# Joining the last steps of a decode kernel to its loop, turning w3 into a moving operand, and sharing semaphores

## The chip, the cores and the metric

The kernel runs on one core of a Trainium2 chip. The profile names its engines PE (TensorE, matrix products; PEld is its loading of weights), DVE (VectorE), ACT (ScalarE), POOL (GpSimd) and SP (SyncE, which issues the loads here); 16 DMA engines move the data. The metric is device time in microseconds (us): the median of repeated executions, of which one per kernel is also profiled. The ratios are the mean time of one kernel's runs over that of the other's runs of the same rounds, so they are not quite the ratio of the medians quoted beside them.

## The reference, cut to what matters

```python
# A: one query position, B=2, 32 heads of 128, 16384 cached positions, bf16
q = (A_x @ wq).reshape(2, 1, 32, 128).transpose(0, 2, 1, 3)
p = softmax(einsum("bhqd,bhkd->bhqk", q, k_cache) * 128 ** -0.5)
a = einsum("bhqk,bhkd->bhqd", p, v_cache) ... @ wo           # wo: 4096 x 1024
# B: mixer and MLP on one position
h  = gelu(layernorm(B_x) @ w1)
hs = concat(shift(h[0:256], +1), shift(h[256:512], -1), ...) @ w2   # shifts along S, padded with zeros
x1 = x + hs
b  = x1 + gelu(layernorm(x1) @ w3) @ w4                       # w3: 1024 x 3584, w4: 3584 x 1024
out = g * a + (1 - g) * b                                     # g = sigmoid(sum(x * gate_w)); both take A_x
```

The K and V caches are 2 x 32 x 16384 x 128 bf16 each. The kernel reads them in 32 tiles each, two heads of one batch row at a time: 8.39 MB per tile.

## The kernel before

Three big buffers ("slots") of 8.39 MB take all large loads in turn: wq, w1 with w2, w3, then K0, K1, V0, K2, V1 and so on, at the end w4 and wo. DVE transposes a K tile in 16 pieces (`turn_k`), PE forms scores from each, a softmax follows, PE multiplies by V. All loads are issued by SP. Straight code does the prologue and K0's scores; a loop of ten turns does 30 tiles; straight code does the last two.

```python
    def linear(w, actT):                        # used for w3: weights stationary
        rows, C = w.shape[1], w.shape[2] // P   # 8, 28
        ps = misc_psum([P, C, B])
        for c in range(C):
            for r in range(rows):
                R.tensor.matmul(ps[:, c, :],
                    lhsT=w[:, r, :].rearrange("k (p c) -> k p c", c=C)[:, :, c],
                    rhs=actT[:, r, :], start=(r == 0), stop=(r == rows - 1))
        return ps
    ...
    load_k(1)
    for k in range(LOOP):                       # LOOP = 30
        load_v(k)
        if k + 2 <= LOOP:
            load_k(k + 2)
    ...
    K = load_k(NT - 1)                          # NT = 32
    V = load_v(NT - 2)
    V_last = load_v(NT - 1, [(sem["free"], 2 * LOOP)])
    note_scores(K)                              # straight code from here on
    w4 = load_pieces(next_slot(), 0, B_w4, W4_SPLIT)      # 14 + 14 rows
    note_outputs(V, NT - 2)
    wo = load_pieces(next_slot(), 0, A_wo, WO_SPLIT)      # 8 8 8 4 2 1 1 rows
    note_softmax()
    note_outputs(V_last, NT - 1)
    st_down(w4)
    wo_stage(wo)
    ...
        with pe.Fori(0, LOOP, NBIG):            # PE's loop, 3 tiles a turn; DVE has its own
            ...
    with tc.tile_critical():
        R.emit([op for op in R.ops[:first_part] if op is not None])
        meet(met[0])
        pe_loop(); dve_loop(); act_steps(); pool_steps()
        meet(met[1])
        R.emit([op for op in R.ops[first_part:] if op is not None])
        nc.sync.wait_ge(stored_sem, 16)
```

## Time and profile before

| | before |
|---|---|
| median, lowest and highest of 3 runs | 1331.46 us, 1331.27, 1331.70 |
| traced span | 1329.4 us |
| loads | 572.53 MB, 434 GB/s from 100 to 1200 us |
| busiest compute engine | PE, 61% |

The prediction below shows how the page is read. It belongs to the list of DMA queues (packets, MB, share of 16 engines); the loads are queue q1, and q8 is a queue on which instructions are fetched, those of PE as the runs below show:

```profile
q8 instruction: 11, 0.18, 0.0%
```

### The profile page before, as it was taken

What the parts mean: (1) busy time and instruction counts of PE and PEld (TensorE: products, weight loads), DVE (VectorE), ACT (ScalarE), POOL (GpSimd) and SP (SyncE); (2) the same over time, 40 slices, a digit from 0 to 9 for tenths busy, and PEclk for the clock granted to TensorE, in tenths of its full rate; (3) what the DMA queues carried; (4) which work ended last, traced back from release to release, by engine and by line L of the source; (5) the groups of instructions that cost most, each with busy time, mean ns of one, the idle gap of its engine ahead of it and who ended that gap; (6) DMA issues with size and microseconds to landing.
All of it is one profiled execution on the core that took longest, in us unless ns stands there. A gap on an engine that the chain in (4) does not pass through costs nothing. (4 is left out here: it accounts for less than half of the span.)

```text
span 1329.4 us, 11487 instructions
## 1 busy us (share of the span) xinstructions
PE 805.7 (61%) x4957; PEld 318.0 (24%) x5011; DVE 761.2 (57%) x1007; ACT 27.2 (2%) x68; POOL 12.8 (1%) x40
## 2 busy tenths in 40 slices
PE   2767676555557655555766555576655556765554
PEld 1522222122222222222222222222212222221222
DVE  2177666655556665555666555566665556666530
ACT  0000000000000000000000000000000000000000
POOL 0000000000000000000000000000000000000000
PEclk9588888777788877778887777888777788877775
DMA  9999999999999999999999999999999999999998
GB/s 405 443 432 426 434 435 442 426 434 434 440 428 440 428 442 426 442 426 442 432 436 426 442 434 434 430 438 438 430 436 432 438 430 442 426 440 428 442 418 342
DMA packets 11121, 572.75 MB, mean 431 GB/s; under 512 B 1239, under 2 KB 1247, under 8 KB 1634
## 3 DMA queue, kind: packets, MB, share of 16 engines
q1 hardware_dynamic: 11100, 572.53, 99.5%
q8 instruction: 11, 0.18, 0.0%
q14 instruction: 4, 0.03, 0.0%
q10 hardware_dynamic: 6, 0.01, 0.0%
HBM read 572.53 MB, written 0.00 MB: 431 GB/s over the span
## 5 line engine op out<-in xcount | busy, mean ns | idle before, releaser
L516 PE MATMUL S<-T,z 128*128 128x512 bf16 x1870 | 553.2, 426 | 301.9 <-DVE T L507 288.1
L507 DVE STREAM_TRANSPOSE T<-slot 128x1024 f32<-128x1024 f32 x480 | 574.5, 1230 | 240.4 <-DVEq L899 190.9
L516 PEld LDWEIGHTS S<-T,z 128*128 128x128 bf16 x1920 | 165.7, 104 | 676.6 <-DVE T L507 516.5
L567 PE MATMUL O<-slot,PT 128*32 128x512 bf16 x1920 | 110.5, 383 | 0.0
L567 PEld LDWEIGHTS O<-slot,PT 128*32 128x32 bf16 x1920 | 69.0, 140 | 41.2 <-issue 13.3
L533 PE MATMUL tot<-rs,ones_f 128*128 128x2 f32 x60 | 17.6, 363 | 73.9 <-DVE rs L558 73.9
L578 DVE TENSOR_SCALAR mix<-O,xmask 128x128 f32<-128x128 f32 x30 | 10.5, 351 | 88.1 <-PE O L567 88.1
L80 PE MATMUL S<-T,z 128*128 128x512 bf16 x124 | 37.2, 432 | 16.4 <-DVE T L80 15.7
L80 DVE STREAM_TRANSPOSE T<-slot 128x1024 f32<-128x1024 f32 x32 | 38.2, 1227 | 11.0 <-DMA slot<-in_A_k_cache_dram 7.1
L550 ACT ACTIVATE mix<-S,nb 128x512 bf16<-128x512 f32 x30 | 20.6, 687 | 1119.5 <-DVE nb L540 1119.5
L586 PE MATMUL oc<-asel,mix 128*128 128x2 f32 x60 | 11.5, 262 | 48.5 <-DVE mix L581 48.5
L525 DVE TENSOR_REDUCE m<-S 128x1 f32<-128x512 f32 x30 | 20.8, 692 | 35.1 <-PE S L516 35.1
L555 DVE STREAM_TRANSPOSE PT<-mix 128x512 bf16<-128x512 bf16 x30 | 21.3, 711 | 25.3 <-ACT mix L550 25.3
L533 PEld LDWEIGHTS tot<-rs,ones_f 128*128 128x128 f32 x60 | 15.0, 312 | 79.7 <-DVE rs L558 79.7
L581 DVE SCALAR_TENSOR_TENSOR mix<-O,xmask,mix 128x128 f32<-128x128 f32 x90 | 31.6, 351 | 3.2
L586 PEld LDWEIGHTS oc<-asel,mix 128*128 128x128 f32 x60 | 8.9, 188 | 62.1 <-DVE mix L581 62.1
L537 DVE TENSOR_REDUCE mx<-mall 64x1 f32<-64x64 f32 x60 | 13.3, 222 | 17.8 <-PE mall L533 17.4
L80 PE MATMUL out_acc<-slot,T 128*17 128x256 bf16 x240 | 14.0, 406 | 15.6 <-DMA slot<-in_A_wo_dram 8.9
L533 PE MATMUL mall<-mix,ones_f 128*128 128x128 f32 x60 | 14.7, 326 | 13.4 <-DVE mix L528 13.4
L80 PEld LDWEIGHTS S<-T,z 128*128 128x128 bf16 x128 | 11.2, 105 | 41.6 <-DVE T L80 27.1
L498 POOL TENSOR_TENSOR z<-qsel,own 128x32 bf16<-128x32 bf16 x30 | 10.1, 338 | 1128.1 <-PE O L567 1128.1
L563 DVE RECIPROCAL rinv<-tot 128x2 f32<-128x2 f32 x30 | 5.1, 171 | 20.4 <-PE tot L533 20.4
(119 smaller groups left out, 163.2 us busy)
## 6 DMA issues: line engine op xcount, KB each, us to landing
slot<-in_B_w_dram SPq DMA_DIRECT2D x1, 7168.0 KB, 48.4
slot<-in_B_w_dram SPq DMA_DIRECT2D x2, 3584.0 KB, 38.3
slot<-in_A_wo_dram SPq DMA_DIRECT2D x3, 2048.0 KB, 42.7
slot<-in_B_w_dram SPq DMA_DIRECT2D x2, 2048.0 KB, 29.2
slot<-in_A_wo_dram SPq DMA_DIRECT2D x1, 1024.0 KB, 48.7
slot<-in_A_k_cache_dram SPq DMA_DIRECT2D x32, 49.3
slot<-in_A_v_cache_dram SPq DMA_DIRECT2D x32, 35.2
slot<-in_A_wo_dram SPq DMA_DIRECT2D x1, 512.0 KB, 49.5
```

The costliest lines, as they stand in the source:

```text
L80: op = Op(engine, lambda: getattr(eng, method)(*args, **kwargs), reads, writes, waits, signal)
L507: return vector.transpose(out=t_tile([P, 2, CJ, 32], FP32, m % 2).rearrange("p w j s -> p j w s"), in_=K[:].bitcast(FP32)[:, m * CW : (m + ...
L516: return tensor.matmul(S, lhsT=z[:, v, NM - 1 - m : NM - 1 - m + P], rhs=Tb[:, v // 2, :, v % 2], start=(m == 0 and v == 0), stop=(m == NM ...
L525: return vector.reduce_max(out=stat["m"][:], in_=S, axis=AX.X)
L533: return tensor.matmul(ps, lhsT=ones_f[:], rhs=src, start=True, stop=True)
L537: return vector.reduce_max(out=stat["mx"][pa, :], in_=mall[pa, pa], axis=AX.X)
L550: return scalar.activation(out=Pr, in_=S, func=ACTF.Exp, bias=stat["nb"][:], scale=scale, accum_out=stat["rs"][:])
L555: return vector.transpose(out=PT[:], in_=Pr)
L567: return tensor.matmul(O[32 * g : 32 * g + 32, :], lhsT=PT[:, m : CJ * 32 : 16], rhs=V[:].rearrange("p (j d) -> p j d", d=Dh)[:, j0 : j0 + ...
L578: return vector.tensor_scalar(out=Os, in0=Ox, scalar1=xmask[:, 0:1], scalar2=None, op0=ALU.mult)
L581: return vector.scalar_tensor_tensor(out=Os, in0=Ox, scalar=xmask[:, x : x + 1], in1=Os, op0=ALU.mult, op1=ALU.add)
L586: return tensor.matmul(oc, lhsT=Os, rhs=asel[:], start=True, stop=True)
```

## The change

Its intent: cover the last two tiles by an eleventh loop turn, with the parts that this turn doesn't need behind two conditionals; compute w3's product with w3 streaming past a small stationary operand (72 matmuls in place of 224); and give the loads a few shared semaphores in place of one each. The section that all engines enter and leave together also gets ACT in place of SP as its boundary engine, the one on which its start and end are synchronized. The core of the diff (cuts marked by "..."):

```diff
-    def linear(w, actT):
-        ... 28 x 8 matmuls of 128x2, w stationary
+    def up_rows(w):
+        HC = FC // 2                                      # 14
+        cols = w.rearrange("k r (g p t j) -> k r g t j p", g=4, p=32, t=2)
+        turned = t_tile([P, 2, HC, 32], FP32)
+        for t in range(2):
+            ps = misc_psum([P, HC, 32])
+            ...                                           # 4 zeroing matmuls
+            for r in range(KC):                           # 8
+                for g in range(4):
+                    R.tensor.matmul(ps[group(g), :, :], lhsT=xnT[:, r, :], rhs=cols[:, r, g, t], ...)
+            R.vector.transpose(out=turned[:, t]..., in_=flat)
...
-    K = load_k(NT - 1)
-    ... straight code for the last two tiles
+    for k in range(LAST + 1):                             # LAST = 30
+        load_v(k, k % NBIG, [(sem["free"], 2 * k - 1)] if k >= 1 else [])
+        if k + 2 < NT:
+            load_k(k + 2)
+    load_v(NT - 1, NBIG - 1, [(sem["free"], 2 * LAST)])
+    w4 = load_pieces(..., [(s, 16) for s in k_in[1:3]], [(sem["free"], 2 * LAST + 1)])
+    wo = load_pieces(..., [...shared semaphores...], [(sem["free"], 2 * LAST + 2)])
...
+    def loop_body(eng, more, scores, outputs, softmax, take_off):
+        for part in (scores, outputs, softmax):
+            part(0)
+        take_off()
+        with eng.If(more):
+            ...                                           # tile 1, and tile 2's scores
+        outputs(NBIG - 1)
+        take_off()
+        with eng.If(more):
+            softmax(NBIG - 1)
+            take_off()
...
-    with tc.tile_critical():
+    with tc.tile_critical(sync_engine=mybir.EngineType.Activation):
```

More of the change, by code (lines that the diff above doesn't have):

```diff
@@ L27, with __init__ @@
 class Op:
-    def __init__(self, engine, emit, reads, writes, waits=(), signal=None):
+    def __init__(self, engine, emit, reads, writes, waits=(), lane=None):
         self.engine, self.emit, self.reads, self.writes = engine, emit, reads, writes
-        self.waits, self.signal = list(waits), signal
+        self.waits, self.lane = list(waits), lane
 class Order:
@@ L70, in box, with add @@
         return name, p0, p1, b0, b1
-    def add(self, engine, method, args, kwargs, waits=(), signal=None, untracked=False):
+    def add(self, engine, method, args, kwargs, waits=(), lane=None, untracked=False):
         reads, writes = [], []
@@ L79, in add @@
         eng = getattr(self.nc, engine)
-        op = Op(engine, lambda: getattr(eng, method)(*args, **kwargs), reads, writes, waits, signal)
+        op = Op(engine, lambda: getattr(eng, method)(*args, **kwargs), reads, writes, waits, lane)
         op.dma = method == "dma_start"
@@ L142, in resolve @@
         self.sems = {
-            f: self.tc.alloc_semaphore(f"{f}_done") for f, ns in self.needed.items() if ns
+            f: self.tc.alloc_semaphore(f"{f}_done") for f in self.needed if not f.startswith("dma")
         }
@@ L149, in target @@
     def target(self, op):
+        if op.dma:
+            return op.lane
         f, n = op.done
-        return self.sems[f], 16 if op.dma else self.rank[f][n]
+        return self.sems[f], self.rank[f][n]
     def emit(self, ops):
@@ L162, in emit @@
             f, n = op.done
-            if op.signal is not None:
-                assert n not in self.needed.get(f, ())
-                ins.then_inc(*op.signal)
+            if op.dma:
+                ins.then_inc(op.lane[0], 16)
             elif n in self.needed.get(f, ()):
-                ins.then_inc(self.sems[f], 16 if op.dma else 1)
-            else:
-                assert not op.dma
+                ins.then_inc(self.sems[f], 1)
 class Engine:
@@ L176, in __getattr__, with call @@
     def __getattr__(self, method):
-        def call(*args, waits=(), signal=None, untracked=False, **kwargs):
-            return self.order.add(self.name, method, args, kwargs, waits, signal, untracked)
+        def call(*args, waits=(), lane=None, untracked=False, **kwargs):
+            return self.order.add(self.name, method, args, kwargs, waits, lane, untracked)
         return call
@@ L294, in load_cache, with load_pieces @@
         return t
-    def load_pieces(t, c0, weights, split):
+    def load_pieces(t, c0, weights, split, lanes, waits=()):
         n = sum(split)
@@ L301, in load_pieces @@
         r0 = 0
-        for k in split:
-            R.sync.dma_start(out=v[:, r0 : r0 + k, :], in_=src[:, r0 : r0 + k, :])
+        for k, lane in zip(split, lanes, strict=True):
+            R.sync.dma_start(
+                out=v[:, r0 : r0 + k, :], in_=src[:, r0 : r0 + k, :], lane=lane, waits=waits
+            )
             r0 += k
@@ L392, in load_x @@
     def load_x():
-        R.scalar.dma_start(out=x_rows[0:B, :], in_=A_x.rearrange("b s d -> (b s) d"))
-        R.scalar.dma_start(out=x_rows[B : B + 1, :], in_=gate_w.rearrange("(o d) -> o d", o=1))
+        R.scalar.dma_start(
+            out=x_rows[0:B, :], in_=A_x.rearrange("b s d -> (b s) d"), lane=(row_in[0], 16)
+        )
+        R.scalar.dma_start(
+            out=x_rows[B : B + 1, :],
+            in_=gate_w.rearrange("(o d) -> o d", o=1),
+            lane=(row_in[1], 16),
+        )
     def spread_x():
@@ L483 @@
     }
-    OT = const([P, (NT + 1) * G], FP32, "OT")
+    OT = const([P, (NT + 2) * G], FP32, "OT")
     PT = const([P, CJ * 32], BF16, "PT")
@@ L724, in half_rows @@
         return rows
-    def linear(w, actT):
-        rows, C = w.shape[1], w.shape[2] // P
-        ps = misc_psum([P, C, B])
-        for c in range(C):
-            for r in range(rows):
-                R.tensor.matmul(
-                    ps[:, c, :],
-                    lhsT=w[:, r, :].rearrange("k (p c) -> k p c", c=C)[:, :, c],
-                    rhs=actT[:, r, :],
-                    start=(r == 0),
-                    stop=(r == rows - 1),
-                )
-        return ps
+    def up_rows(w):
[4 more added lines that the diff above has]
+            ps = misc_psum([P, HC, 32])
+            flat = ps.rearrange("p j k -> p (j k)")
+            for g in range(4):
+                zero_rows(flat, g, HC * 32)
+            for r in range(KC):
+                for g in range(4):
+                    R.tensor.matmul(
+                        ps[group(g), :, :],
+                        lhsT=xnT[:, r, :],
+                        rhs=cols[:, r, g, t],
+                        start=False,
+                        stop=(r == KC - 1),
+                        skip_group_check=True,
+                    )
+            R.vector.transpose(out=turned[:, t].rearrange("p j k -> p (j k)"), in_=flat)
+        return turned.rearrange("p t j k -> p (t j) k")[:, :, 0:B]
     xnT = const([P, KC, B], BF16, "xnT")
@@ L770, in st_up @@
     def st_up(w3):
-        h2 = t_tile([P, FC, B], FP32)
-        R.vector.tensor_copy(out=h2, in_=linear(w3, xnT))
-        gelu(h2, h2T[:], omg_bc[:])
+        gelu(up_rows(w3), h2T[:], omg_bc[:])
     def st_down(w4):
@@ L782, in wo_stage @@
         gated = const([P, B, H], BF16, "gated")
+        R.vector.tensor_copy(
+            out=OT[:, G * (NT - 1) : G * NT], in_=OT[:, G * NT : G * (NT + 1)]
+        )
         for b in range(B):
@@ L799, in wo_stage, with load_k, load_v @@
             add_row_product(Q[:, r, :], wo[:, r, :], last=(r == 31))
-    LOOP = (NT - 2) // NBIG * NBIG
-    assert LOOP == NT - 2
+    LAST = NT - 2
+    assert LAST % NBIG == 0
     sem = {
         n: tc.alloc_semaphore(n)
-        for n in ("to_pe", "to_dve", "own_dve", "to_act", "from_act", "to_pool", "from_pool", "free")
-    }
+        for n in ("to_pe", "to_dve", "own_dve", "to_act", "from_act", "to_pool", "from_pool")
+        + ("free", "met")
+    }
+    row_in = [tc.alloc_semaphore(f"row_in{n}") for n in range(2)]
+    w_in = [tc.alloc_semaphore(f"w_in{n}") for n in range(5)]
     k_in = [tc.alloc_semaphore(f"k_in{n}") for n in range(NBIG)]
     v_in = [tc.alloc_semaphore(f"v_in{n}") for n in range(NBIG)]
-    met = [tc.alloc_semaphore(f"met{n}") for n in range(2)]
+    k_slot, v_slot = {}, {}
+    def load_k(j):
+        waits = [(sem["free"], 2 * (j - NBIG) + 2)] if j >= NBIG else []
+        k_slot[j] = load_cache(
+            A_k_cache, j, waits=waits, lane=(k_in[(j - 1) % NBIG], 16), untracked=True
+        )
+    def load_v(j, turn, waits):
+        v_slot[turn] = load_cache(A_v_cache, j, waits=waits, lane=(v_in[turn], 16), untracked=True)
     load_x()
-    wq_slot = next_slot()
-    wq = load_pieces(wq_slot, 0, A_wq, [KC])
+    wq = load_pieces(next_slot(), 0, A_wq, [KC], [(w_in[0], 16)])
     w12_slot = next_slot()
-    w1 = load_pieces(w12_slot, 0, B_w1, [KC])
-    w2 = load_pieces(w12_slot, KC * D, B_w2, [KC])
-    w3 = load_pieces(next_slot(), 0, B_w3, [KC])
+    w1 = load_pieces(w12_slot, 0, B_w1, [KC], [(w_in[1], 16)])
+    w2 = load_pieces(w12_slot, KC * D, B_w2, [KC], [(w_in[2], 16)])
+    w3 = load_pieces(next_slot(), 0, B_w3, [KC], [(w_in[3], 16)])
     spread_x()
@@ L826 @@
     compute_gate()
-    K = load_cache(A_k_cache, 0)
+    K = load_cache(A_k_cache, 0, lane=(w_in[4], 16))
     st_mix(w1, w2)
@@ L833 @@
     build_z(R.gpsimd, 1)
-    k_slot, v_slot = {}, {}
-    def load_k(j):
-        waits = [(sem["free"], 2 * (j - NBIG) + 2)] if j >= NBIG else []
-        if j > LOOP:
-            return load_cache(A_k_cache, j, waits=waits)
-        k_slot[j] = load_cache(
-            A_k_cache, j, waits=waits, signal=(k_in[(j - 1) % NBIG], 16), untracked=True
-        )
-    def load_v(j, waits=None):
-        if waits is None:
-            waits = [(sem["free"], 2 * j - 1)] if j >= 1 else []
-        if j >= LOOP:
-            return load_cache(A_v_cache, j, waits=waits)
-        v_slot[j] = load_cache(
-            A_v_cache, j, waits=waits, signal=(v_in[j % NBIG], 16), untracked=True
-        )
     load_k(1)
-    for k in range(LOOP):
-        load_v(k)
-        if k + 2 <= LOOP:
+    for k in range(LAST + 1):
+        load_v(k, k % NBIG, [(sem["free"], 2 * k - 1)] if k >= 1 else [])
+        if k + 2 < NT:
             load_k(k + 2)
+    load_v(NT - 1, NBIG - 1, [(sem["free"], 2 * LAST)])
+    w4 = load_pieces(
+        next_slot(), 0, B_w4, W4_SPLIT, [(s, 16) for s in k_in[1:3]], [(sem["free"], 2 * LAST + 1)]
+    )
+    wo = load_pieces(
+        next_slot(),
+        0,
+        A_wo,
+        WO_SPLIT,
+        [(k_in[0], 16), (v_in[0], 16), (v_in[1], 16)] + [(s, 32) for s in w_in[:4]],
+        [(sem["free"], 2 * LAST + 2)],
+    )
     R.meet()
@@ L861 @@
     R.meet()
-    K = load_k(NT - 1)
-    V = load_v(NT - 2)
-    V_last = load_v(NT - 1, [(sem["free"], 2 * LOOP)])
-    note_scores(K)
-    w4 = load_pieces(next_slot(), 0, B_w4, W4_SPLIT)
-    note_outputs(V, NT - 2)
-    wo = load_pieces(next_slot(), 0, A_wo, WO_SPLIT)
-    note_softmax()
-    note_outputs(V_last, NT - 1)
     st_down(w4)
@@ L875 @@
     R.vector.tensor_copy(out=rows, in_=out_acc)
-    stored = R.sync.dma_start(
-        out=out.rearrange("b s (g n) -> g (b s) n", g=NQ), in_=rows[0 : P : APART, :]
+    R.sync.dma_start(
+        out=out.rearrange("b s (g n) -> g (b s) n", g=NQ),
+        in_=rows[0 : P : APART, :],
+        lane=(row_in[0], 32),
     )
@@ L884, in __init__, with next @@
             self.eng, self.s, self.n = eng, s, 0
-        def next(self, ins=None, by=1):
-            self.n += by
+        def next(self, ins=None):
+            self.n += 1
             if ins is None:
@@ L896, in take_off @@
             self.eng.wait_ge(self.s, self.n).then_inc(self.s, -self.n)
+            self.n = 0
     def take(eng, s, n):
@@ L902, in pe_loop @@
         pe = nc.tensor
-        with pe.Fori(0, LOOP, NBIG):
-            got = Count(pe, sem["to_pe"])
-            for t in range(NBIG):
-                for m in range(NM):
-                    for v in range(4):
-                        ins = score(pe, m, v)
-                        if v == 0:
-                            got.next(ins)
-                        if v == 3:
-                            ins.then_inc(sem["to_dve"], 1)
-                take(pe, v_in[t], 16)
-                for m in range(NM):
-                    for g in range(4):
-                        ins = weigh(pe, v_slot[t], m, g)
-                        if m == 0 and g == 0:
-                            ins.then_inc(sem["to_pool"], 1)
-                ins.then_inc(sem["to_dve"], 1)
-                got.next(join_heads(pe)).then_inc(sem["to_dve"], 1)
-                got.next(sum_rows(pe, mall, mdiag)).then_inc(sem["to_dve"], 1)
-                got.next(sum_rows(pe, tot, stat["rs2"][:])).then_inc(sem["to_dve"], 1)
-                take(pe, sem["from_pool"], 1)
-            got.take_off()
+        got = Count(pe, sem["to_pe"])
@@ new lines, in scores, with outputs @@
+        def scores(t):
+            for m in range(NM):
+                for v in range(4):
+                    ins = score(pe, m, v)
+                    if v == 0:
+                        got.next(ins)
+                    if v == 3:
+                        ins.then_inc(sem["to_dve"], 1)
+        def outputs(t):
+            take(pe, v_in[t], 16)
+            for m in range(NM):
+                for g in range(4):
+                    ins = weigh(pe, v_slot[t], m, g)
+                    if m == 0 and g == 0:
+                        ins.then_inc(sem["to_pool"], 1)
+            ins.then_inc(sem["to_dve"], 1)
+            got.next(join_heads(pe)).then_inc(sem["to_dve"], 1)
@@ L926, in dve_loop, with softmax @@
+        def softmax(t):
+            got.next(sum_rows(pe, mall, mdiag)).then_inc(sem["to_dve"], 1)
+            got.next(sum_rows(pe, tot, stat["rs2"][:])).then_inc(sem["to_dve"], 1)
+            take(pe, sem["from_pool"], 1)
+        with pe.Fori(0, LAST + 1, NBIG) as k:
+            loop_body(pe, k < LAST, scores, outputs, softmax, got.take_off)
     def dve_loop():
         dve = nc.vector
-        with dve.Fori(0, G * LOOP, G * NBIG) as place:
-            got = Count(dve, sem["to_dve"])
-            mine = Count(dve, sem["own_dve"])
-            exp_done = Count(dve, sem["from_act"])
-            for t in range(NBIG):
-                take(dve, k_in[t], 16)
-                for m in range(NM):
-                    ins = turn_k(dve, k_slot[t + 1], m)
-                    if m >= 2:
-                        got.next(ins)
-                    ins.then_inc(sem["to_pe"], 1)
-                got.skip(1)
-                got.next(top(dve)).then_inc(sem["own_dve"], 1)
-                mine.next().then_inc(sem["free"], 1)
-                got.next(pick_head(dve, 0)).then_inc(sem["own_dve"], 1)
-                for x in range(1, 4):
-                    mine.next(pick_head(dve, x)).then_inc(
-                        sem["own_dve"] if x < 3 else sem["to_pe"], 1
-                    )
-                got.next(put_head(dve, bass.DynSlice(place + G * t, G))).then_inc(sem["free"], 1)
-                spread_top(dve).then_inc(sem["to_pe"], 1)
-                got.next(head_top(dve, 0))
-                head_top(dve, 1).then_inc(sem["own_dve"], 1)
-                mine.next(bias(dve)).then_inc(sem["to_act"], 1)
-                exp_done.next(turn_p(dve))
-                split_sums(dve).then_inc(sem["to_pe"], 1)
-                got.next(invert(dve))
-            got.take_off()
-            mine.take_off()
-            exp_done.take_off()
@@ new lines, in dve_loop, with scores @@
+        counts = got, mine, exp_done = [
+            Count(dve, sem[n]) for n in ("to_dve", "own_dve", "from_act")
+        ]
+        def scores(t):
+            take(dve, k_in[t], 16)
+            for m in range(NM):
+                ins = turn_k(dve, k_slot[t + 1], m)
+                if m >= 2:
+                    got.next(ins)
+                ins.then_inc(sem["to_pe"], 1)
+            got.skip(1)
+            got.next(top(dve)).then_inc(sem["own_dve"], 1)
+            mine.next().then_inc(sem["free"], 1)
@@ new lines, in outputs, with softmax @@
+        def outputs(t):
+            got.next(pick_head(dve, 0)).then_inc(sem["own_dve"], 1)
+            for x in range(1, 4):
+                mine.next(pick_head(dve, x)).then_inc(sem["own_dve"] if x < 3 else sem["to_pe"], 1)
+            got.next(put_head(dve, bass.DynSlice(place + G * t, G))).then_inc(sem["free"], 1)
+        def softmax(t):
+            spread_top(dve).then_inc(sem["to_pe"], 1)
+            got.next(head_top(dve, 0))
+            head_top(dve, 1).then_inc(sem["own_dve"], 1)
+            mine.next(bias(dve)).then_inc(sem["to_act"], 1)
+            exp_done.next(turn_p(dve))
+            split_sums(dve).then_inc(sem["to_pe"], 1)
+            got.next(invert(dve))
@@ new lines, in take_off @@
+        def take_off():
+            for c in counts:
+                if c.n:
+                    c.take_off()
+        with dve.Fori(0, G * (LAST + 1), G * NBIG) as place:
+            loop_body(dve, place < G * LAST, scores, outputs, softmax, take_off)
+    def loop_body(eng, more, scores, outputs, softmax, take_off):
[3 more added lines that the diff above has]
+        with eng.If(more):
+            for t in range(1, NBIG - 1):
+                for part in (scores, outputs, softmax):
+                    part(t)
+            scores(NBIG - 1)
+            take_off()
[3 more added lines that the diff above has]
+            softmax(NBIG - 1)
+            take_off()
@@ L959, in act_steps @@
     def act_steps():
-        for k in range(LOOP):
+        for k in range(LAST + 1):
             exps(nc.scalar)._wait_ge(sem["to_act"], k + 1).then_inc(sem["from_act"], 1)
     def pool_steps():
-        for k in range(LOOP):
-            build_z(nc.gpsimd, k + 2)._wait_ge(sem["to_pool"], k + 1).then_inc(sem["from_pool"], 1)
-    def meet(s):
+        for k in range(LAST + 1):
+            build_z(nc.gpsimd, min(k + 2, NT - 1))._wait_ge(sem["to_pool"], k + 1).then_inc(
+                sem["from_pool"], 1
+            )
@@ L968, in meet @@
+    def meet(value):
         for e in COMPUTE:
-            getattr(nc, e).drain().then_inc(s, 1)
+            getattr(nc, e).drain().then_inc(sem["met"], 1)
         for e in COMPUTE:
-            getattr(nc, e).wait_ge(s, len(COMPUTE))
+            getattr(nc, e).wait_ge(sem["met"], value)
     R.resolve()
-    stored_sem = tc.alloc_semaphore("stored")
-    stored.signal = (stored_sem, 16)
-    with tc.tile_critical():
+    with tc.tile_critical(sync_engine=mybir.EngineType.Activation):
         R.emit([op for op in R.ops[:first_part] if op is not None])
-        meet(met[0])
+        meet(len(COMPUTE))
@@ L982 @@
         pool_steps()
-        meet(met[1])
+        meet(2 * len(COMPUTE))
         R.emit([op for op in R.ops[first_part:] if op is not None])
-        nc.sync.wait_ge(stored_sem, 16)
+        nc.sync.wait_ge(row_in[0], 32)
 _INS = ['A_x', 'A_k_cache', 'A_v_cache', 'A_wq', 'A_wo', 'B_x', 'B_w1', 'B_w2', 'B_w3', 'B_w4', 'gate_w']
```

## The prediction

> **What bounds the kernel now.** I read the profile page first: busy shares, slices, DMA queues.
>
> ```profile
> PE 805.7 (61%) x4957; PEld 318.0 (24%) x5011; DVE 761.2 (57%) x1007; ACT 27.2 (2%) x68; POOL 12.8 (1%) x40
> DMA  9999999999999999999999999999999999999998
> GB/s 405 443 432 426 434 435 442 426 434 434 440 428 440 428 442 426 442 426 442 432 436 426 442 434 434 430 438 438 430 436 432 438 430 442 426 440 428 442 418 342
> q1 hardware_dynamic: 11100, 572.53, 99.5%
> ```
>
> No compute engine is over 61% busy, while the DMA row is full in every slice but the last, and the loads' queue fills 99.5% of what 16 engines can give over the span. The kernel is one stream of 572.53 MB: 64 tiles of K and V of 8.39 MB (537 MB) and 35.6 MB of weights. To split the span into the stream and what lies outside it, I asked for busy time in six stretches (PE, PEld, DVE, ACT, POOL, then granted clock, DMA share, GB/s):
>
> ```profile
> 0.00:2.00 2.00, 0.00 (x0) 0.00 (x0) 0.44 (x5) 0.25 (x1) 0.70 (x6) 1.00 0.22 68
> 100.00:1200.00 1100.00, 681.86 (x3836) 258.31 (x3884) 671.81 (x836) 21.78 (x56) 9.80 (x29) 0.81 1.00 434
> 1325.00:1329.40 4.40, 0.29 (x4) 0.10 (x4) 0.42 (x1) 0.00 (x0) 0.00 (x0) 0.74 0.00 1
> ```
>
> The head is about 2 us. The middle runs at 434 GB/s with a DMA share of 1.00, so a tile takes 8.39 MB / 434 GB/s = 19.3 us. After the last weight lands there are 4.4 us: last matmuls, a copy, the store, the closing barrier. 572.53 MB / 434 GB/s = 1319 us, plus 2 and 4.4, is 1326 us; the remaining 4 us to 1329.4 is rate lost in the first and last stretches. The untraced runs have a median of 1331.46 us.
>
> So the question for every part of the change is: does the loads' queue ever run dry, or does the head or tail change? The page's issue rows (KB where given, median us from issue to landing) and the waits of the issuing engine answer the first half.
>
> ```profile
> slot<-in_A_k_cache_dram SPq DMA_DIRECT2D x32, 49.3
> slot<-in_A_v_cache_dram SPq DMA_DIRECT2D x32, 35.2
> ```
> ```profile
> SPq L80 <- DVEq L889: 983.8, 30, 34.0
> SPq L80 <- DVE OT L589: 140.4, 30, 4.7
> ```
>
> A V load lands 35.2 us after it is issued but needs only 19.3 us of stream, so it stood 15.9 us in the queue behind others: it could have been issued 15.9 us later at no cost. For K the slack is 49.3 - 19.3 = 30.0 us. The issuing engine's 984 us of waiting for a free slot are thus not lost stream time. The compute chain has slack of its own: in the timeline around 205 us a tile takes from 205.56 (first transpose of K) to 237.2 (reciprocal), 31.6 us, and the next starts at 244.18, when its K has landed: 38.6 us per pair of tiles against 31.6 of work, **7 us spare per tile**.
>
> [...] the new w3 operand steps by 28 bf16 elements = 56 bytes. Nothing in the trace shows such a moving operand, only such a stationary one. [...] The trace before has a branch per three tiles, but DVE waits for K there anyway.
>
> **The change part by part.**
>
> 1. *w3 as moving operand.* Now 224 matmuls with 2 columns each and 224 loads of 128x128 weights:
>
> ```profile
> 55.08 14.63 PE L80 MATMUL mall<-xnT,slot 128*128 128x2 bf16 x224
> 69.75 0.33 SPq L80 DMA_DIRECT2D slot<-in_A_v_cache_dram  x1
> 69.75 0.22 DVE L80 COPY T<-mall 128x56 f32<-128x56 f32 x1 [15.71 <-PE mall L80]
> ```
>
> They go; in their place come two halves of 4 zeroing and 32 moving matmuls of 448 columns, plus a DVE transpose of 128x448 each. The nearest row is the query projection, whose 32 matmuls of 128x512 in four column groups took 3.58 us[...]. 3.58 x 448/512 = 3.1 us, zeroing 0.6 us, transposes about 0.6 us each (the 128x512 one of P took 0.71): 2 x (3.1 + 0.6) + 0.6 (the other transpose overlaps) = 8 us instead of 14.9. If 56-byte steps halve the read rate, 2 x (6.2 + 0.6) + 0.6 = 14 us. So the stage ends 1 to 7 us earlier. K0's scores (first transpose now at 71.7) gain at most 4.5 of that, as K0 lands at about 2 + 28.3/0.434 = 67.2 us. What is it worth? It lies in the prologue, beside the stream. The first V load behind it, issued at 69.75, has 36.7 MB ahead of it (wq, w1, w2, w3, K0, K1), so its transfer starts at 2 + 36.7/0.434 = 87 us: slack 17 us. The tightest issue of all comes next: V1 at 121.9 us, with 53.5 MB ahead of it (V0 and K2 more), so it is wanted at 2 + 53.5/0.434 = 125 us: **3 us of slack**. The change widens this. Worth: 0 us.
>
> 2. *The last steps in the loop.* K31's scores, V30's and V31's outputs and one softmax move from straight code into an eleventh loop turn. Same matmuls and transposes, same loads in the same order into the same slots. Two conditionals per turn on PE and DVE, 11 turns, plus draining and resetting counters three more times per turn. I choose 1 us per conditional with its resets, an estimate (the counting-down branches in the trace are under 0.2 us each): about 2 us per three tiles against 3 x 7 us spare. Worth: 0.
>
> 3. *The final loads wait differently.* w4's first half was issued at 1258.98 us, the second at 1267.4, as K31's halves were transposed; now both wait for the row maximum of K31, about 1271.9. V31's transfer holds the queue to 1287.3, so 15 us remain. wo was issued piecewise from 1271.9 to 1275.7; now after V30's heads are written, about 1277, while w4 streams to 1305.7: 29 us remain. Worth: 0.
>
> 4. *The meeting of engines moves* from before K31 to after V31's heads (1295.95 now). About 1 us of drain delays w4's products from 1297.2 to about 1298.3; they take 3.2 us, and the second half of w4 lands only at 1305.7. One more 2-column copy joins wo's preparation, also before 1305. Worth: 0.
>
> 5. *Shared semaphores, another boundary engine.* The loads keep 16 increments each. SP no longer owns the section's boundary, ACT does. In the head SP's first load comes 0.2 us after its own signal; now it waits for ACT's. In the tail SP hands over to ACT[...]. Worth: between -0.3 and +0.4 us.
>
> Sum: 1331.46 + 0 + about 0.04 = **1331.5 us**.
>
> **Rivals.** (a) *The strided w3 is far slower*, four times: 2 x (12.5 + 0.6) + 0.6 = 27 us, 12 later than now. It eats the 3 us at V1 and the stream stands for about 9 us: 1340 us, still within 2%. For it: the 56-byte step. Against: weight loads with that step took 172 ns each but came every 14.63/224 = 65 ns, so 128 such reads in 65 ns do not look crippled. (b) *Branches stall on instruction fetch*, so that DVE or PE becomes the bound: it would take over 21 us per turn; at, say, 25 us, 11 x 4 = 44 us more, 1375 us. Against: 7 us per tile and 16 us of queue stand before it. (c) *Less work at the start shortens the run*: were the 7 us on the path, 1325 us. Against: the queue is full all that time (440 GB/s from 25 to 100 us). (d) *The tail grows*: a late meeting pushes w4's and wo's products behind the last landing. It would have to be over 7 us late; then about 1 us per us.
>
> **Range and chances.** The three runs lie within 0.43 us. Boundary effects are under half a us each way; rival (a) in a mild form adds a few us on one side, a stream rate differing by 0.1% from run to run gives 1.3 us. Eight in ten: 1330.3 to 1333.0. Two per cent is 27 us: for faster the stream itself would have to shrink, 0.01; for slower, (b), 0.01; same 0.98.
>
> **What would show it.** In the changed profile: 572.5 MB still, DMA row full, 434 GB/s in the middle; V loads still some 35 us from issue to landing (under 19.5 would mean a dry queue); w3's stage ending 1 to 7 us earlier, with the tightest V issue before 122 us; the gap from the last wo landing to the end still 4.4 us within 0.3; w4's first products near 1298 and finished before 1305. What would make me wrong: a stretch with a DMA share well under 1 at the start or at a loop turn, or DVE no longer waiting for K at each tile.

The 0.04 for the boundary engine stands without its ground, a cost of the hand-over in the tail that was assumed; in the changed kernel's trace ACT goes on 0.03 us after SP there. The 1 us per conditional and the 1 us of drain in part 4 were my estimates: the new conditionals' branches took 0.04 to 0.21 us, the meeting held DVE for 0.62 us, and w4's first products began at 1296.35 us, not near 1298. That 56-byte steps could halve the rate, or cut it to a quarter (rival a), and that branches could stall on fetches (rival b), were suppositions; what was measured of them comes below.

## The result, and the profile after

| | before | after |
|---|---|---|
| median of 6 runs | 1331.38 us | 1329.58 us |
| lowest, highest | 1331.23, 1331.70 | 1329.53, 1329.99 |
| traced span | 1329.4 us | 1327.8 us |

The ratio is 0.9987, with a 95% interval from 0.9974 to 1.0: within 2%, the same, as foreseen. But the two sets of runs don't overlap, and 1329.58 lies below my range (1330.3 to 1333.0): 1.8 us went that I had no term for. Most of what I had looked for is there. The stretches (PE, PEld, DVE, ACT, POOL busy, granted clock, DMA share, GB/s) of the changed kernel:

```profile
0.00:2.00 2.00, 0.00 (x0) 0.00 (x0) 0.42 (x5) 0.19 (x1) 0.70 (x6) 1.00 0.30 100
100.00:1200.00 1100.00, 680.98 (x3836) 257.78 (x3883) 671.55 (x834) 21.78 (x56) 9.84 (x29) 0.81 1.00 434
```

The middle is the same 434 GB/s. Its issue rows say the same of the queue:

```profile
slot<-in_A_k_cache_dram SPq DMA_DIRECT2D x32, 49.3
slot<-in_A_v_cache_dram SPq DMA_DIRECT2D x32, 35.1
```

V still waits 15.8 us in the queue beyond its own transfer. The w3 stage, from its timeline:

```profile
56.26 6.32 PE L82 MATMUL mall<-slot,xnT 128*2 128x448 bf16 x32
62.59 6.28 PE L82 MATMUL tot<-slot,xnT 128*2 128x448 bf16 x32
68.91 0.33 SPq L82 DMA_DIRECT2D slot<-in_A_v_cache_dram  x1
```

It took 6.3 us per half, my slow case (6.2), and freed its slot for V0 0.8 us before the old one. So the prologue got hardly shorter, and the stream was full in any case. But that my slow case fits is partly luck. It doubles 3.58 us, the time of 32 matmuls of 128x512 from the query projection, which I took for their time at a low clock; the next 32, of the same shape and contiguous too, took 1.90:

```profile
22.86 3.58 PE L80 MATMUL spare<-slot,xT 128*2 128x512 bf16 x32 [11.32 <-DMA slot<-in_A_wq_dram]
26.64 1.90 PE L80 MATMUL mall<-slot,xT 128*2 128x512 bf16 x32
```

The trace's clock records begin only between the two, at 26.6 us, so the clock of the first 32 isn't shown. In the changed kernel's w3 stage, groups of four matmuls start every 0.76 us, whether the granted clock (third column from the end) is 0.50 or 1.00:

```profile
57.03:57.79 0.76, 0.76 (x8) 0.12 (x4) 0.00 (x0) 0.00 (x0) 0.00 (x0) 0.50 0.20 86
59.33:60.08 0.75, 0.75 (x8) 0.12 (x4) 0.00 (x0) 0.00 (x0) 0.00 (x0) 1.00 0.20 87
```

Scaled to 448 columns, the contiguous matmuls would take 3.1 us at the slower pace and 1.7 at the faster: the strided ones took 2 and 3.8 times as long. No run varied the step alone, so that the step causes it is my reading.

What differs is the very end. In the kernel before, the last weight loads landed and freed PE like this, in the timeline:

```profile
1324.65 0.10 PEld L80 LDWEIGHTS out_acc<-slot,T 128*17 128x17 bf16 x4 [0.50 <-DMA slot<-in_A_wo_dram]
1325.26 0.10 PEld L80 LDWEIGHTS out_acc<-slot,T 128*17 128x17 bf16 x4 [0.51 <-DMA slot<-in_A_wo_dram]
```

and in the changed one like this:

```profile
1323.20 0.10 PEld L82 LDWEIGHTS out_acc<-slot,T 128*17 128x17 bf16 x4 [0.52 <-DMA slot<-in_A_wo_dram]
1323.82 0.10 PEld L82 LDWEIGHTS out_acc<-slot,T 128*17 128x17 bf16 x4 [0.52 <-DMA slot<-in_A_wo_dram]
```

The same last row of wo comes 1.44 us earlier. Of the 1.90 us between the two profiled runs (1331.44 and 1329.54), 1.43 lie before the last landing (1325.21 and 1323.78), 0.2 between it and the end of the span, and 0.27 outside the traced span. These landing times come from the trace's own records of semaphore signals, of which `prof` has no view.

**The stream did not shrink; its end got sharper.** The last four microseconds before that landing, in the kernel before:

```profile
1321.20:1322.20 1.00, 1.00 (x20) 0.43 (x12) 0.00 (x0) 0.00 (x0) 0.00 (x0) 0.50 0.91 365
1322.20:1323.20 1.00, 0.44 (x12) 0.27 (x12) 0.00 (x0) 0.00 (x0) 0.00 (x0) 0.50 0.66 252
1323.20:1324.20 1.00, 0.80 (x24) 0.26 (x12) 0.00 (x0) 0.00 (x0) 0.00 (x0) 0.76 0.17 66
1324.20:1325.20 1.00, 0.52 (x12) 0.10 (x4) 0.00 (x0) 0.00 (x0) 0.00 (x0) 1.00 0.08 31
```

and in the changed kernel:

```profile
1319.80:1320.80 1.00, 0.93 (x20) 0.30 (x11) 0.00 (x0) 0.00 (x0) 0.00 (x0) 0.50 0.98 406
1320.80:1321.80 1.00, 0.51 (x12) 0.38 (x16) 0.00 (x0) 0.00 (x0) 0.00 (x0) 0.50 1.00 399
1321.80:1322.80 1.00, 0.77 (x20) 0.15 (x12) 0.00 (x0) 0.00 (x0) 0.00 (x0) 0.50 0.65 252
1322.80:1323.80 1.00, 0.76 (x12) 0.10 (x4) 0.00 (x0) 0.00 (x0) 0.00 (x0) 0.50 0.26 98
```

The last column is GB/s, the one before it the share of the 16 DMA engines that is busy. Before, for the last 2 us it is 0.17 and 0.08: one to three engines still have work, and the others have run out. PE went on only after the last of a load's signals (1325.21, and its weight load at 1325.26), so the last two stragglers held the end.

**Who made them late?** Each of these loads signals 16 times in the trace; I read this as once per DMA engine, and in a_actsem below, with one of the 16 signals outstanding, the DMA share is 0.06, one sixteenth. The landing records give, for each load, how long before the last of the 16 each of the others signalled. For the kernel before, around the moment when it goes wrong (us, sorted):

```
V31, landed 1287.27:          0 .01 .06 .08 .14 .17 .21 .26 .29 .81 1.08 1.17 1.42 1.66 1.67 1.68
w4, 1st half, landed 1297.20: 0 1.46 1.48 1.54 1.59 1.64 1.66 1.71 1.77 2.29 2.52 2.62 2.88 3.10 3.11 3.12
last row of wo, 1325.21:      0 .11 1.48 1.52 1.56 1.57 1.62 1.64 1.74 2.37 2.50 2.59 2.84 3.08 3.09 3.10
```

At 1287 nine engines come within 0.3 us of each other and hold the end together. Ten microseconds later one of them is alone, 1.46 us behind. Between the two, at 1291.1 us, lies one 16384-byte packet of the queue q8. I then matched all landing rows with all q8 packets. In the kernel before, such packets start at 31.5, 58.7, 65.7, 77.9, 118.9, 148.0 and 181.8 us, then 1263.7, 1291.1, 1309.3 and 1323.2. Each of the first ten falls between two landings between which one engine more becomes about 1.5 us later than the rest; the eleventh changes no landing any more. The packets' own records last only 0.88 to 0.96 us. Between neighbours, outside the loop's later turns, lie 143 to 407 recorded PE instructions; that it is PE's program being fetched is shown by a_pad1 and b_pad1 below, where 256 PE instructions more give one packet more. In the loop of these two kernels there are no fetches after its first turn: none from 181.8 to 1263.7 us in the kernel before, none from 191.2 to 1301.2 in the changed one.

The first eight fetches hit engines that had not been hit, so they only fill up a late group, which lags the rest by 1.5 us after the very first. (The ninth engine of the row at 1287 got there otherwise: two 8192-byte packets of another instruction queue, q14, at 38.2 and 199.3 us, each made it about 0.7 us later.) The ninth, at 1291.1, hits an engine of the late group: from then on one engine is 3 us behind the engines that were never hit, and 1.5 us behind the group. In the changed kernel's page:

```profile
q1 hardware_dynamic: 11100, 572.53, 99.6%
q8 instruction: 8, 0.13, 0.0%
```

Eight fetches, not eleven: six up to 191.2 us, then at 1301.2 and 1317.4. There is no ninth. Its last landing shows it:

```
last row of wo, 1323.78:      0 .10 .11 .20 .22 .23 .24 .33 .34 1.22 1.28 1.40 1.48 1.55 1.77 1.83
```

Nine engines end together, again eight and the one that q14 hit twice. The program for PE got shorter in two places: w3's stage needs 304 fewer PE instructions (72 matmuls and weight loads in place of 224 of each), and the joined loop takes the last two tiles' straight code away. How many instructions the second saves I did not count.

### The profile page after: what moved, and what is told of

Same layout as the page of the kernel before. It is cut to its first block, busy times and chain, and to the rows that moved or that the text cites. A ratio compares the mean times of both kernels' runs of the same rounds, so it can differ in the third digit from the quotient of the medians. Undisturbed runs are those within 1.5% of the kernel's fastest.

```text
span 1327.8 us, 11371 instructions
## 1 busy us (share of the span) xinstructions
PE 801.6 (60%) x4806; PEld 305.4 (23%) x4859; DVE 762.7 (57%) x1009; ACT 27.2 (2%) x68; POOL 13.2 (1%) x41
## 5 line engine op out<-in xcount | busy, mean ns | idle before, releaser
L526 PEld LDWEIGHTS S<-T,z 128*128 128x128 bf16 x1984 | 171.1, 104 | 698.0 <-DVE T L517 532.5
L577 PE MATMUL O<-slot,PT 128*32 128x512 bf16 x2048 | 119.6, 387 | 7.2 <-PEq L921 7.2
L577 PEld LDWEIGHTS O<-slot,PT 128*32 128x32 bf16 x2048 | 74.0, 140 | 52.2 <-issue 23.0
L560 ACT ACTIVATE mix<-S,nb 128x512 bf16<-128x512 f32 x31 | 21.3, 687 | 1158.3 <-DVE nb L550 1158.3
L599 DVE TENSOR_TENSOR OT<-oc,rinv 128x2 f32 x32 | 5.1, 159 | 15.2 <-PE oc L596 15.2
```

The costliest lines, as they stand in the source:

```text
L526: return tensor.matmul(S, lhsT=z[:, v, NM - 1 - m : NM - 1 - m + P], rhs=Tb[:, v // 2, :, v % 2], start=(m == 0 and v == 0), stop=(m == NM ...
L560: return scalar.activation(out=Pr, in_=S, func=ACTF.Exp, bias=stat["nb"][:], scale=scale, accum_out=stat["rs"][:])
L577: return tensor.matmul(O[32 * g : 32 * g + 32, :], lhsT=PT[:, m : CJ * 32 : 16], rhs=V[:].rearrange("p (j d) -> p j d", d=Dh)[:, j0 : j0 + ...
```

## The experiments

**Theory F**: a fetch of PE's program takes time from one DMA engine and makes it about 1.5 us later; up to eight fetches cost the end one such lag, the ninth costs it another 1.5 us. **Rivals**: the prologue was on the path after all (W), the joined loop by itself shortens the tail (J), the boundary engine or the semaphores do (B), every fetch costs its share (N). All kernels ran five times beside the kernel before, and all gave a correct result.

**a_pad1: one fetch more, nothing else.** In the changed kernel, the eight matmuls that spread x are repeated 17 times, with the same result, while PE waits for wq:

```diff
-        for r in range(KC):
+        for r in [r for _ in range(17) for r in range(KC)]:
             R.tensor.matmul(xg_ps[:, r, :], lhsT=x_rows[:, r:D:KC], ...
```

> The changed kernel with 128 more tiny matmuls (256 PE instructions with their weight loads) that repeat the spreading of x with the same result, in the 11 us in which PE waits for wq. Theory F (instruction fetch): a 16 KB fetch of PE's program goes through one DMA engine and makes that engine about 1.5 us later; up to 8 fetches hit 8 different engines and all cost the end only once; the ninth hits an engine that is late already, and the last load, which needs all 16 engines, lands 1.5 us later. The page should show 9 packets of the instruction queue where it showed 8, and the time 1329.6 + 1.4 = 1331.0 us (1330.6 to 1331.4). Rival W (the time saved is prologue work that was on the path, or chance): the padding lies in idle time, so 1329.6 us, within 0.3.

Measured: 1330.82 us (1330.60 to 1330.93), 1.24 us more than the changed kernel; ratio to before 0.9996. The added work did lie in idle time:

```profile
10.49 8.32 PE L82 MATMUL spare<-ident_b,T 3*128 3x3 bf16 x136 [10.49 <-DMA T<-in_gate_w_dram]
```

It was over at 18.8 us, 5 us before wq's products (24.1 us in this run). Its queues:

```profile
q8 instruction: 9, 0.15, 0.0%
```

The ninth packet starts at 1318.2 us, and the landing rows turn over there:

```
wo, 2nd piece, landed 1314.18:  0 .26 .28 .29 .38 .46 .49 .69 .79 1.41 ...
wo, 3rd piece, landed 1320.24:  0 1.24 1.48 1.48 1.54 1.62 1.69 1.89 1.98 2.64 ...
```

The extra fetch, at 19.8 us, also made wq land 1.4 us later than in the changed kernel (24.10 against 22.73), a rival to be excluded. The landings exclude it: wo's 2nd piece comes 0.2 us later than in the changed kernel (1314.18 against 1313.94), its 3rd, behind the ninth packet, 1.4 us later (1320.24 against 1318.80). So 256 instructions in idle time cost 1.24 us, and at the end, 1300 us after they ran. W falls.

**a_w3old: the changed kernel with the old w3 stage.**

```diff
     def st_up(w3):
-        gelu(up_rows(w3), h2T[:], omg_bc[:])
+        h2 = t_tile([P, FC, B], FP32)
+        R.vector.tensor_copy(out=h2, in_=linear(w3, xnT))
+        gelu(h2, h2T[:], omg_bc[:])
```

> The changed kernel with w3 as stationary operand again (224 matmuls and weight loads): 304 PE instructions more. Theory F: 9 instruction packets, 1331.0 us (1330.6 to 1331.4), although the tail is the joined one. Rival J (joining the loop itself shortens the tail): 1329.6 us. Rival W (the w3 stage's 1 us was on the path): 1330.5 us.

Measured: 1330.84 us (1330.61 to 1331.03), nine packets, the ninth at 1318.3 us. The joined loop without the shorter w3 stage gives 0.5 us, not 1.8. J falls, and the time is that of a_pad1, whose w3 stage is the new one: in these two, the number of instructions counts, not which. (Of the 0.5 us, only 0.14 lies before the last landing. And not all of this run's delay is the ninth's: its q14 packet at 1284.5 us hit an engine of the late group too and put the next landing back by some 0.5 us.)

**b_w3: the kernel before with the new w3 stage alone** (the reverse edit).

> The kernel before with w3 as moving operand alone: 304 PE instructions fewer. Theory F: 10 instruction packets (or 9), of which the ninth still comes before the last load ends, so no gain: 1331.3 us, within 0.4. Rival W: the gain of the change comes with w3: 1329.6 to 1330.5 us.

Measured: 1331.55 us (1331.08 to 1331.60), ratio 1.0. Nine packets, the ninth at 1309.1 us: no gain at all. So the two parts don't add: w3 alone -0.2 us of gain, the join with the rest of the change 0.5, all together 1.8. Only together do they go below nine fetches.

**b_bound and a_bound: the boundary engine alone.**

```diff
-    with tc.tile_critical():                                                # b_bound: kernel before
+    with tc.tile_critical(sync_engine=mybir.EngineType.Activation):
-    with tc.tile_critical(sync_engine=mybir.EngineType.Activation):         # a_bound: changed kernel
+    with tc.tile_critical():
```

> The kernel before with ACT as the section's boundary engine instead of SP, alone. Theory F: 11 instruction packets as before; only the tail behind the last landing changes, by about -0.15 us (4.17 before, 4.02 in the changed kernel), so 1331.2 us, within 0.2. Rival B (the boundary makes the whole difference): 1329.6 us.

> The changed kernel with SP as the section's boundary engine again, alone. Theory F (the ninth instruction fetch makes most of the difference): still 8 instruction packets, so only the tail behind the last landing grows, by the 0.15 to 0.25 us that the boundary saved in the kernel before: 1329.8 us (1329.6 to 1330.0). Rival B (the boundary engine is needed for the gain): 1331 us.

Measured: b_bound 1331.13 us (1331.07 to 1331.35), eleven packets; a_bound 1329.87 us (1329.84 to 1330.14), eight. In both directions the boundary is worth about 0.25 to 0.3 us, and is not needed for the rest. But it isn't all in the tail, as I had expected: from the last landing to the end of the span there are 4.16 us before and 4.08 in b_bound, 3.97 after and 4.14 in a_bound; the landing itself came 0.23 earlier and 0.42 later. One run each, and the runs of a_bound and of the changed kernel fall into two clusters some 0.3 and 0.4 us apart, so what the boundary changes stays open.

**a_sems: 14 semaphores more that nobody uses**, allocated in the changed kernel.

> The changed kernel with 14 more semaphores that nobody uses, about as many as the kernel before had. Between the traced span and the measured time lie 2.0 us in the kernel before (2.0 and 2.35 in its variants) and 1.75 to 1.85 in the changed one and its variants. If the number of semaphores makes that difference: 1329.9 us, and 2.0 us outside the span. If not: 1329.6 us and 1.75.

Measured: 1329.73 us (1329.71 to 1329.81). 0.15 us more, but the time outside the traced span stayed at 1.8 us. Not what either reading foresaw; the number of semaphores doesn't explain the 0.27 us outside the span, and that remainder stays open.

**a_now2mm: less prologue work, no fetch spared that matters.** With one position, all shifts of h bring in zeros, so the product with w2 is exactly zero:

```diff
-        hs = half_rows(w2, shT)
-        ... 16 matmuls, x1 = xT + hs
+        R.vector.tensor_copy(out=x1[:], in_=xT[:])
```

> The changed kernel without the products with w2 (exactly zero for one position, so the result stays right) but with its load: about 100 PE instructions fewer and some 7 us less work in the prologue. Theory F: the eighth fetch costs nothing as it is, and a fetch fewer or later gains nothing; nor does the shorter prologue: 1329.6 us (1329.3 to 1329.9), 7 or 8 packets. Rival N (each fetch costs its share): up to 1.5 us less. Rival W (prologue on the path): several us less.

Measured: 1329.53 us (1329.46 to 1329.65), eight packets, the last two at 1308.5 and 1322.4. The last packet changes no landing, so seven fetches count here against eight, and the time is the same. The prologue's work is off the path, and below nine the fetches are not worth a share each: N falls on this side.

**b_pad1: the padding of a_pad1 in the kernel before.**

> The kernel before with the same 256 PE instructions of padding in PE's idle time before wq lands: 12 instruction packets instead of 11. Theory F with 8 engines in turn: the ninth to the twelfth hit four different engines that were hit once, so the end is delayed once, as before: 1331.4 us (1331.0 to 1331.7). Rival N (each fetch that hits a late engine adds its 1.5 us to the end): 1332.8 us.

Measured: 1331.58 us (1331.36 to 1332.46), twelve packets. The ninth now comes at 1262.7 us and again one engine falls behind, 1.4 us behind the next at the following landing; the tenth and eleventh hit other engines of the late group and add nothing. N falls on this side too, by the median; one of the five runs reached 1332.46.

**Instructions on an idle engine.** Does ACT's program cost the same? The first attempt put 64 no-operations behind each of ACT's 31 exponentials.

> The changed kernel with 64 no-operations behind each of ACT's 31 exponentials, 1984 instructions on an engine that is 2% busy. If only PE's program costs DMA time, or an idle engine's instructions are free: 1329.6 us. Theory F for every engine: about 15 more packets of 8 KB on the instruction queues, each making one DMA engine 0.7 us later (as the four such packets do now); if they go round over the engines, the end comes 0.5 to 2 us later: 1330.1 to 1331.6 us.

It measured 1329.55 us and told nothing: ACT's trace holds two no-operations, as many as the changed kernel's, so the added ones never reached the program. The third used semaphore instructions, which nothing waits for:

```diff
         for k in range(LAST + 1):
             exps(nc.scalar)._wait_ge(sem["to_act"], k + 1).then_inc(sem["from_act"], 1)
+            for n in range(64):
+                nc.scalar.wait_ge(sem["met"], 4).then_inc(junk, 1)
```

> The changed kernel with 64 semaphore instructions (a wait that is always met, an increment that nobody reads) behind each of ACT's 31 exponentials: 1984 instructions more on an engine that is 2% busy, after no-operations were dropped by the build and activations were refused. If only PE's program costs DMA time: 1329.6 us. Theory F for every engine: about 15 more instruction packets of 8 KB, 0.7 us of one DMA engine each; over several engines in turn 0.5 to 2 us: 1330.1 to 1331.6 us.

Measured: 1337.45 us (1337.25 to 1337.57), 7.9 us more than the changed kernel, ratio to before 1.0046. It is the clearest of all runs. Its queues, of which q14 had 4 packets of instructions before:

```profile
q8 instruction: 8, 0.13, 0.0%
q14 instruction: 19, 0.16, 0.0%
```

Fifteen packets of 8192 bytes more, most of them 75 to 78 us apart. I had expected them to go round over the engines; they hardly do. The first few hit at least two engines, but from 359.7 us on thirteen packets in a row make one and the same engine 0.6 to 0.8 us later. At the end it is alone, for 8 us (DMA share and GB/s in the last columns):

```profile
1324.00:1326.00 2.00, 0.00 (x0) 0.00 (x0) 0.00 (x0) 0.00 (x0) 0.00 (x0) 0.50 0.06 25
1326.00:1328.00 2.00, 1.24 (x24) 0.87 (x28) 0.00 (x0) 0.00 (x0) 0.00 (x0) 0.50 0.06 25
1328.00:1330.00 2.00, 1.46 (x29) 0.57 (x20) 0.00 (x0) 0.00 (x0) 0.00 (x0) 0.50 0.06 25
```

0.06 of 16 engines is one engine, and 25 GB/s is near one engine's share of the middle's 434 (27). Its last signal (1331.68) comes 7.76 us behind that of the next engine. The middle of this run still shows a DMA share of 1.00 and 434 GB/s, so the loss can't be seen there:

```profile
100.00:1200.00 1100.00, 676.07 (x3766) 255.17 (x3813) 668.12 (x827) 21.80 (x56) 9.55 (x28) 0.81 1.00 434
```

**a_nomix: fewer bytes.** If the stream is the bound, only bytes help. For one position the result doesn't depend on w1 and w2 at all, so this version neither loads them nor multiplies by them (it is valid for one position alone, which it asserts):

```diff
-    w1 = load_pieces(w12_slot, 0, B_w1, [KC], [(w_in[1], 16)])
-    w2 = load_pieces(w12_slot, KC * D, B_w2, [KC], [(w_in[2], 16)])
...
-        ... layernorm, h1, gelu, hs
+        R.vector.tensor_copy(out=x1[:], in_=xT[:])
```

> The changed kernel without the loads and products of w1 and w2, on which the result doesn't depend for one position: 4.19 MB fewer. If the stream alone bounds the kernel, 4.19 / 0.434 = 9.7 us less: 1319.9 us (1319.3 to 1320.5), and faster than both kernels. If the prologue had hidden stalls of its own, another number.

Measured: 1320.23 us (1320.01 to 1320.36), ratio to before 0.9916 (0.9903 to 0.993): 9.4 us less than the changed kernel for an expected 9.7, and faster than both kernels, though still within 2%. Its middle runs at the same rate, with seven instruction packets:

```profile
100.00:1200.00 1100.00, 682.90 (x3857) 255.40 (x3855) 664.50 (x833) 22.56 (x58) 9.81 (x29) 0.81 1.00 434
```

The runs that load the same bytes and leave ACT's program as it is, with the q8 packets of the profiled run and its last landing:

| kernel | q8 packets | the ninth at, us | last landing, us | median, us |
|---|---|---|---|---|
| before | 11 | 1291.1 | 1325.21 | 1331.38 |
| b_bound | 11 | 1292.0 | 1324.98 | 1331.13 |
| b_pad1 | 12 | 1262.7 | 1325.10 | 1331.58 |
| b_w3 | 9 | 1309.1 | 1324.93 | 1331.55 |
| a_w3old | 9 | 1318.3 | 1325.07 | 1330.84 |
| a_pad1 | 9 | 1318.2 | 1324.98 | 1330.82 |
| after | 8 | none | 1323.78 | 1329.58 |
| a_bound | 8 | none | 1324.20 | 1329.87 |
| a_now2mm | 8 | none | 1323.87 | 1329.53 |
| a_sems | 8 | none | 1323.86 | 1329.73 |
| a_actnop | 8 | none | 1323.77 | 1329.55 |

Every kernel with nine or more lands its last weights between 1324.9 and 1325.2 us; every one with eight between 1323.8 and 1324.2. b_bound is the least clean: there two engines are some 1 us late beyond the group from 190 us on, after several had slipped at 147 us without a packet, and the ninth moves the last signal by only 0.5 us. The trace has no number of the engine that a packet ran on, so in which order fetches go over the engines is not shown; what is shown, by the landing rows, is that the first eight hit engines not hit before and that the ninth, in six kernels of six, hits a late one.

## Why the prediction was right or wrong

**Right**: the bound (one full stream), and the sum's zeros for the joined loop's branches and for the later issue of w4 and wo. w4 was issued at 1271.4 and wo at 1276.4 us, as foreseen, and neither ran the queue dry. The w3 stage took the slow case's 6.3 us per half instead of 6.2, partly by luck (see above), and freed its slot 0.8 us earlier, just short of the 1 to 7; that this was worth nothing fits a_now2mm, where more work was removed. Two small readings were off: K0 landed at 70.3 us and not at about 67.2, which left its scores 1.4 us to gain and not 4.5, and most of PE's counting-down branches took 0.21 to 0.23 us, not under 0.2. Neither bore on the sum.

**Right, with its size**: the boundary engine, which I put between -0.3 and +0.4 us; b_bound and a_bound measured -0.25 and -0.29 for it. But I entered it in the sum as +0.04, by taking the hand-over in the tail for a cost, which no trace showed.

**Wrong**: the line "Worth: 0" under parts 1 and 2, as far as it followed from "same loads in the same order". I counted what the change does to the loads and to the engines' work, and left out what it does to the program itself. The fetches of instructions delay the DMA engines that carry the data: here by about 1.5 us of one engine for each packet of 16384 bytes. 304 instructions fewer at w3 and the straight code of two tiles less are three fetches fewer, and with the ninth gone the last landing came forward: of its 1.43 us, 1.20 go with this fetch, as a_pad1 measured (1324.98 against 1323.78). The page had said it: 11 packets on the instruction queue. I had even thought of instruction fetch, but only for branches (rival b), with no trace that showed such a stall.

The step behind it is the opening one: "1319 us, plus 2 and 4.4, is 1326 us; the remaining 4 us to 1329.4 is rate lost in the first and last stretches". I noted 4 us that the stream's rate doesn't explain and went on without asking where they were. By the same sum wq should have landed at 21.3 us and w2 at 31.0; they landed at 22.81 and 33.99, so 3 us had gone by then, half of it with the first fetch at 31.5 us. A part of the 4 us is the lag of the slowest DMA engine, 3.1 us behind the first at the last landing before and 1.8 us after. A mean over 16 engines hides it, as the DMA share of 1.00 in a_actsem shows.

**The range** followed from that: "boundary effects are under half a us each way" left 1.2 us below the centre, and the missing fetch alone is worth 1.2, with the boundary's 0.25 to 0.3 besides. Rival (c), less work at the start shortening the run, was rightly set aside. The rival that came true was not on the list: a transfer that nobody issued.

**Open**: which DMA engine a fetch uses, and why it makes that engine 1.5 us later when its own packet lasts 0.9; what the boundary engine changes; and the 0.27 us between the traced span and the measured time (2.06 us before, 1.79 after). It isn't the semaphores (a_sems: 1.79), nor the boundary (b_bound: 2.07, a_bound: 1.79), and it returned in a_nomix (2.07).

## What to carry to other kernels

In this kernel, bound by DMA, the end was set by the slowest of the 16 engines (3.1 us behind the first before, 1.8 after), and fetches of PE's and ACT's programs delayed them (1.24 us for the ninth packet in a_pad1, 7.9 us for fifteen in a_actsem). In another: count the instruction packets on the page, and look at how far apart the 16 engines land, not only at the mean share. Straight code cost DMA time here even on an engine that is busy 2% of the time (a_actsem), while PE's loop in these two kernels fetched nothing after its first turn (a_nomix fetched one packet in a later turn, at 425.4 us). Parts of a change need not add: here the new w3 stage alone, and the rest without it, stayed at nine fetches, and only both together went below.
